# Leftover rows of two experts in one tile of an expert layer

## The chip, the cores and the metric

The kernel runs on one core of a Trainium2 chip. The metric is the device time of one execution in microseconds, here the median of three timed runs; beside them one execution was taken by the hardware profiler. The engines are named as the profile does: PE is TensorE's matmuls, PEld its weight loads, DVE VectorE, ACT ScalarE, POOL GpSimd, SP SyncE, and a q behind a name is that engine's queue.

## The reference

Three layers follow each other: a gated linear attention over 4 batches, 8 heads, 768 steps and 48 numbers a head; a SiLU layer of 384 to 2048 to 384 on the 3072 tokens; and a layer of 8 experts in which each token goes to the one expert with the highest score. The last is what the change touches:

```python
N, D, E, F = (3072, 384, 8, 1024)
expert_idx = np.argmax(logits, axis=1)
for e in range(E):
    mask = expert_idx == e
    h = np.maximum(x[mask] @ w1[e], 0.0)
    out[mask] = gate_w[mask, None] * (h @ w2[e])
```

## The kernel before

Every product of the two matmul layers is made of three fp16 products (high by high, high by low, low by high), so that it is nearly as exact as fp32. The attention, the SiLU layer and the conversion of all weights run first, interleaved, up to about 600 us. All expert weights then lie in SBUF as pairs of fp16 (`w1s`, `w2s`).

`route` (line 900) scores 128 tokens at a time and scatters each token's row into a DRAM buffer `xs_d` in which every expert has a region of its own: the row as two halves of fp16, and ten numbers of metadata (its place in the output, its scale, eight scores). The expert layer then works on tiles of 128 rows of one expert each. Eight tiles (`KEARLY`) are listed by `early` (line 1085) from the tokens routed before the last block, whole tiles only. `tile_list` (line 1096) lists the others when all tokens are counted: `tiles_of` rounds each expert's remaining rows up to whole tiles, and `listing` makes the first row (`idx`) and the expert (`ei`) of 23 places; places past the end of the list point to dummy rows. An expert's last tile is thus partly empty: its rows past the end are padding (`write_pads`, line 1112) that the output scatter leaves out.

29 tiles (`NSTAT`, 8 + 21) always run; two more are behind a branch (line 1357) that is entered when the list is longer than 21 (`extra`, line 1103). A tile goes through these steps:

- `prep_load` (line 1125): SyncE loads the first row's number into a register (line 1130), transposes the 128 rows from DRAM into `xT` (line 1135, three buffers) and loads the metadata `mt` (line 1136, four buffers).
- `prep_fac` (line 1145): the softmax weight of each row, on ACT and DVE.
- `expert1` (line 1165), once for each half of 1024 hidden columns: PE makes nine matmuls of 512 columns into `hp` (line 1183), 18 a tile, with the rows as the stationary operand and the expert's weights streaming; ACT and DVE split the result into two fp16 parts (lines 1189, 1190); `send` (line 1161) has SyncE transpose them back into SBUF. The destinations are `g3` and `hb` for even tiles and two parts of `work` for odd ones.
- `expert2` (line 1196): 24 matmuls of 384 columns into `po` (line 1209), 12 from each half of the hidden columns; ACT scales the result (line 1217) and GpSimd scatters the rows into the output (line 1220).

The expert of a tile is in a register of PE, so each matmul's weights are addressed at run time. In the loop of line 1340, turn j issues the load of tile j+3, the weights of rows of tile j+2, the first stage of tile j+1 and the second stage of tile j. The order on each engine is set when the program is built, by a planner that runs the instructions through a model of their times and picks, among those that are ready, the earlier one in the code. The queues work strictly in that order; a SyncE instruction that waits holds up all behind it.

Of the kernel before, what the change touches and what calls it, by code (L numbers as in the profile page):

```python
# [272 lines left out]
def attention_silu_moe_kernel(  # L273
# [14 lines left out]
    nc = tc.nc  # L288
    B, H, S, D = q.shape
    NT, DM = out.shape  # L290
# [11 lines left out]
    AHEAD = 2  # L302
    POOLW2 = {(c, e) for c in range(4, KE) for e in (0, 4)}
    GATE = mybir.DependencyClass.Sync
    NLIST = NTILE - KEARLY
    NSTAT = NTILE - 2
    CAP = NT + 128
    DUMMY = E * CAP
    ROW = DM + E + 2
# [11 lines left out]

    def guard(kind, thr=0.0, op=ALU.is_lt):
        if kind not in guards:
            width = {"decay": 2 * NCH, "nat": NCH, "finite": 160}.get(kind, 16)
            t = const.tile([128, width], FP32, name=f"guard_{kind}")
            nc.vector.memset(t, 2.0 * thr if op == ALU.is_lt else 0.0)
            guards[kind] = [t, 0, thr, op]
        g = guards[kind]
        g[1] += 1
        return g[0][:, g[1] - 1:g[1]]  # L330
# [41 lines left out]
    if True:  # L372
# [662 lines left out]
        es = const.tile([128, E], FP32, name="es")  # L1035
        idx0 = const.tile([128, KEARLY], I32, name="idx0")
        ei0 = const.tile([128, KEARLY], I32, name="ei0")
        idx = const.tile([128, NLIST], I32, name="idx")
        ei = const.tile([128, NLIST], I32, name="ei")
        ends = const.tile([128, E], I32, name="ends")  # L1040
        extra = const.tile([128, 1], I32, name="extra")
# [54 lines left out]
        def tile_list():  # L1096
            cn = totals(NCH, "cn1")
            nc.vector.scalar_tensor_tensor(
                out=ends, in0=iota8, scalar=float(CAP), in1=cn, op0=ALU.mult, op1=ALU.add
            )  # L1100
            nc.vector.tensor_sub(out=cn, in0=cn, in1=es)
            tl, tcum = tiles_of(cn, 127.0)
            nc.vector.tensor_scalar(
                out=extra, in0=tcum[:, E - 1:E], scalar1=float(NSTAT - KEARLY), scalar2=None, op0=ALU.is_gt
            )
            base = m2.tile([128, E], FP32, tag="base", name="base1", bufs=1)
            nc.vector.scalar_tensor_tensor(out=base, in0=iota8, scalar=float(CAP), in1=es, op0=ALU.mult, op1=ALU.add)
            listing(tl, tcum, base, NLIST, idx, ei)

        early_loads, pads = [], []  # L1110

# [10 lines left out]

        tl_ = {}

        def prep_load(j):
            d = tl_[j] = {}
            d["x"] = xT = m2.tile([128, 2 * KD, 128], FP16, tag="row", name="xT", bufs=3)
            mt = m2.tile([128, ROW - DM], FP32, tag="mt", name="mt", bufs=4)
            src = idx0[0:1, j:j + 1] if j < KEARLY else idx[0:1, j - KEARLY:j - KEARLY + 1]
            r = nc.values_load(  # L1130
                src, engines=sp, min_val=0, max_val=DUMMY,
                skip_runtime_bounds_check_because="a tile starts inside an expert's rows or at the dummy rows",
            )
            loads = [
                nc.sync.dma_start_transpose(out=xT, in_=xs_d.bitcast(FP16)[bass.ds(r, 128), 0:2 * DM]),
                nc.sync.dma_start(out=mt, in_=xs_d[bass.ds(r, 128), DM:]),
            ]
            if j < KEARLY:
                for ins in loads:
                    for other in scattered[NCH - TPB:] + pads:  # L1140
                        tc.declare_no_dep(ins.ins, other.ins, reason="early tiles hold tokens of earlier blocks only")
                early_loads.extend(loads)
            d["m"] = mt
# [21 lines left out]
        def expert1(j, i, keep=False):  # L1165
            d = tl_[j]
            if i == 0:
                d["e"] = nc.values_load(
                    ei0[0:1, j:j + 1] if j < KEARLY else ei[0:1, j - KEARLY:j - KEARLY + 1],
                    engines=[mybir.EngineType.PE], min_val=0, max_val=E - 1,  # L1170
                    skip_runtime_bounds_check_because="the chip clamps the index to an expert",
                )
                d["hs"] = work[:, 1024 * (j % 2):1024 * (j % 2 + 1)].bitcast(FP16).rearrange(
                    "p (i s f) -> p i s f", i=2, s=2)
                odd = work[:, 2048:3072].bitcast(FP16)
                d["hT"] = (odd[:, 0:1024], odd[:, 1024:2048]) if j % 2 else (g3[:, 0:1024], hb)
            xT = d["x"]
            fs = slice(i * 512, (i + 1) * 512)
            hp = ps_h.tile([128, 512], FP32, tag="h", name="hp2")
            n = 0  # L1180
            for c in range(KD):
                for a, w in ((c, "h"), (KD + c, "h"), (c, "l")):
                    nc.tensor.matmul(  # L1183
                        out=hp, lhsT=xT[:, a, :], rhs=w1s[w][c][:, bass.ds(d["e"], 1), fs],
                        start=(n == 0), stop=(n == 3 * KD - 1),
                    )
                    n += 1
            hs = d["hs"][:, i]
            nc.scalar.activation(out=hs[:, 0], in_=hp, func=ACTF.Relu)  # L1189
            nc.vector.scalar_tensor_tensor(  # L1190
                out=hs[:, 1], in0=hp, scalar=0.0, in1=hs[:, 0], op0=ALU.max, op1=ALU.subtract
            )
            if not keep:
                send(j, i)

        def expert2(j, part=None):
            d = tl_[j] if part == 0 else tl_.pop(j)
            hT = d["hT"]
            if part != 1:
                d["o"] = (  # L1200
                    bank([128, 512], FP32, "po") if j < 2 else ps_o.tile([128, 512], FP32, tag=f"o{j % 2}", name="po")
                )[:, 0:DM]
            po = d["o"]
            order = [[0, 1, 2, 3], [4, 5, 6, 7]] if part is None else [[[0, 1, 2, 3], [4, 6]], [[5, 7]]][part]
            n, total = (3 * 6 if part == 1 else 0), 3 * KE
            for group in order:
                for a, w in ((0, "h"), (0, "l"), (4, "h")):
                    for c in group:
                        nc.tensor.matmul(
                            out=po, lhsT=hT[c // 4][:, (a + c % 4) * 128:(a + c % 4 + 1) * 128], rhs=w2s[w][c][:, bass.ds(d["e"], 1), :],  # L1210
                            start=(n == 0), stop=(n == total - 1),
                        )
                        n += 1
            if part == 0:
                return
            ob = m2.tile([128, ROW], FP32, tag="sq", name="ob", bufs=1)[:, 0:DM]
            nc.scalar.activation(  # L1217
                out=ob, in_=po, func=ACTF.Copy, scale=d["fac"], accum_out=guard("finite", 0.0, ALU.not_equal)
            )
            nc.gpsimd.indirect_dma_start(  # L1220
                out=out[:, :], out_offset=bass.IndirectOffsetOnAxis(ap=d["row"], axis=0),
                in_=ob, in_offset=None, bounds_check=NT - 1, oob_is_err=False,
            )
# [113 lines left out]
        send(3, 1)  # L1337
        tile_list()
        write_pads()
        for j in range(2, NSTAT):  # L1340
            if j + 3 < NSTAT:
                prep_load(j + 3)
            if j + 2 < NSTAT:
                prep_fac(j + 2)
            if 2 < j and j + 1 < NSTAT:
                expert1(j + 1, 0)
                expert1(j + 1, 1)
            if j + 2 == NSTAT:
                bad = const.tile([128, len(guards) + 1], FP16, name="bad")
                n_fin = guards["finite"][1]  # L1350
                for i, kind in enumerate(guards):
                    check(i, kind, 0, guards[kind][1])
            expert2(j)
# [1 line left out]
    more = nc.values_load(extra[0:1, 0:1], min_val=0, max_val=NTILE,  # L1355
                          skip_runtime_bounds_check_because="at most NTILE tiles in the list")
    with tc.If(more > 0):
        for j in range(NSTAT, NTILE):
            prep_load(j)
            prep_fac(j)  # L1360
            expert1(j, 0)
            expert1(j, 1)
            expert2(j)
# [43 lines left out]
```

## Time and profile before

| | us |
|---|---|
| median of 3 timed runs (838.42 to 839.84) | 839.2 |
| the profiled execution | 834.05 |
| its span, first to last instruction | 832.4 |

The page of the profile gives, for each engine, the busy time and its share of the span, and in 40 slices of the span the busy tenths (9 is 90% or more) and TensorE's granted clock in tenths of full speed. The views of the trace used below are the table by stretches (busy time of each engine in a stretch), the timeline (instructions in order, equal neighbours merged, with a count at the end), the groups by line, and the waits. Matmuls follow each other before the one ahead has ended, so the duration of one is longer than the distance between two.

### The profile page before, as it was taken

The numbers are of one execution on the slowest core, as the hardware profiler recorded it, in microseconds if no ns is written. First come the engines' busy times: TensorE is split into PE (matmuls) and PEld (weight loads), VectorE is DVE, ScalarE is ACT, GpSimd is POOL, SyncE is SP. The second block draws the span as 40 slices with busy tenths as digits, with TensorE's granted clock in tenths as the row PEclk, the third lists the DMA queues.
The fourth block names the chain that finished last, engine by engine and source line by source line (L and its number), as shares of the span: only waits on it lengthen the run. The fifth ranks groups of instructions, "written<-read, shape, count | busy, mean of one in ns | idle before, by whom it ended". The sixth has DMA issues, their size and how long they took to land. (4 is left out here: it accounts for less than half of the span.)

```text
span 832.4 us, 16583 instructions
## 1 busy us (share of the span) xinstructions
PE 779.0 (94%) x5488; PEld 492.0 (59%) x5488; DVE 500.0 (60%) x1444; ACT 431.4 (52%) x931; POOL 248.2 (30%) x335
## 2 busy tenths in 40 slices
PE   6879799999999999998999988989799999999996
PEld 5756577667667666665657655555344555555553
DVE  7799963767777977786677576466543222222221
ACT  2456664656675846666556575667542222222221
POOL 3342311534453554444222121131343111111111
PEclk9959899999999999999999999999999999999998
DMA  9997132144445454534521345345588666555663
GB/s 188 256 289 201 48 49 48 50 93 80 96 106 118 89 147 100 112 96 86 106 79 47 97 135 159 90 134 153 166 160 188 115 112 121 103 118 120 109 117 61
DMA packets 244028, 98.66 MB, mean 119 GB/s; under 512 B 224969, under 2 KB 233326, under 8 KB 243808
## 3 DMA queue, kind: packets, MB, share of 16 engines
q1 hardware_dynamic: 240288, 86.31, 48.8%
q0 software_dynamic: 3648, 11.18, 3.9%
q8 instruction: 51, 0.84, 0.4%
q14 instruction: 41, 0.34, 0.1%
HBM read 58.40 MB, written 12.36 MB: 85 GB/s over the span
## 5 line engine op out<-in xcount | busy, mean ns | idle before, releaser
L870 PE MATMUL hp<-w2h,wi_h 128*128 128x384 f16 x576 | 146.2, 331 | 7.4 <-ACT w2l L877 5.3
L893 PE MATMUL o<-wo_h,w2l 128*128 128x392 f16 x528 | 147.1, 333 | 6.0 <-DVE wo_h L569 3.6
L1190 DVE SCALAR_TENSOR_TENSOR work<-hp,work 128x512 f16<-128x512 f32 x58 | 39.9, 690 | 121.6 <-ACT work L1189 121.5
L893 PEld LDWEIGHTS <-w2l 128*128 128x128 f16 x792 | 75.5, 98 | 57.9 <-issue 6.9
L870 PEld LDWEIGHTS <-wi_h 128*128 128x128 f16 x768 | 74.0, 98 | 54.7 <-issue 10.1
L1183 PE MATMUL hp<-w1h,xT 128*128 x348 | 103.5, 379 | 2.4 <-DVE work L1190 2.4
L870 PE MATMUL hp<-w2h,wi_l 128*128 128x384 f16 x288 | 94.8, 330 | 0.1
L893 PE MATMUL o<-wo_l,w2l 128*128 128x392 f16 x264 | 87.8, 332 | 0.0
L1183 PEld LDWEIGHTS <-xT 128*128 128x128 f16 x522 | 50.9, 98 | 60.7 <-issue 3.0
L1220 POOL DMA_INDIRECT out_dram<-ob,mt x29 | 28.3, 976 | 176.3 <-ACT ob L1217 171.7
L1189 ACT ACTIVATE work<-hp 128x512 f16<-128x512 f32 x58 | 34.4, 595 | 68.4 <-PE hp L1183 61.6
L893 PE MATMUL o<-wo_h,g 128*128 128x392 f16 x240 | 67.0, 329 | 1.2 <-DVE g L879 1.1
L879 DVE SCALAR_TENSOR_TENSOR w2l<-w2l 128x384 f16<-128x384 f32 x88 | 51.1, 583 | 27.8 <-ACT w2l L878 27.5
L1183 PE MATMUL hp<-w1l,xT 128*128 x174 | 66.0, 379 | 0.0
L877 ACT ACTIVATE w2l<-hp 128x384 f32<-128x384 f32 x88 | 42.4, 483 | 36.0 <-PE hp L870 31.8
L692 PE MATMUL sc<-Q,K 64*128 64x128 f32 x384 | 54.8, 307 | 1.7 <-DVE state L817 1.0
L692 PEld LDWEIGHTS sc<-Q,K 64*128 64x128 f32 x384 | 46.0, 207 | 14.0 <-issue 7.1
L870 PEld LDWEIGHTS <-wi_l 128*128 128x128 f16 x384 | 37.8, 99 | 24.3 <-issue 1.0
L698 POOL TENSOR_SCALAR_AFFINE_SELECT S<-S 128x512 f32<-128x512 f32 x48 | 36.5, 764 | 45.7 <-ACT S L697 45.3
L878 ACT ACTIVATE w2l<-w2l 128x384 f16<-128x384 f32 x88 | 45.7, 521 | 5.8 <-PE o L893 4.1
L870 PE MATMUL hp<-w2l,wi_h 128*128 128x384 f16 x192 | 48.2, 326 | 0.0
L893 PEld LDWEIGHTS <-g 128*128 128x128 f16 x360 | 34.0, 98 | 23.2 <-DVE g L879 2.2
(276 smaller groups left out, 1603.7 us busy)
## 6 DMA issues: line engine op xcount, KB each, us to landing
work<-in_moe_w_dram SPq DMA_DIRECT2D x24, 512.0 KB, 3.8
work<-in_moe_w_dram SPq DMA_DIRECT2D x30, 384.0 KB, 3.5
w1h<-in_moe_w_in_dram SPq DMA_DIRECT2D x6, 768.0 KB, 5.4
nat_a<-in_alpha_dram SPq DMA_DIRECT2D x23, 192.0 KB, 3.2
nat_k<-in_k_dram SPq DMA_DIRECT2D x23, 192.0 KB, 2.8
nat_q<-in_q_dram SPq DMA_DIRECT2D x23, 192.0 KB, 3.2
nat_v<-in_v_dram SPq DMA_DIRECT2D x23, 192.0 KB, 2.9
w1h<-in_moe_w_out_dram SPq DMA_DIRECT2D x5, 768.0 KB, 7.2
```

The lines of the kernel that those rows point to most:

```text
L692: nc.tensor.matmul(out=sc[i][:, p, :], lhsT=d["K"][r, p, :], rhs=d["Q"][r, p, :], start=True, stop=True)
L698: nc.gpsimd.affine_select(out=s, in_=s, pattern=[[0, NPAIR], [1, 128]], compare_op=ALU.is_ge, fill=0.0, base=0, channel_multiplier=-1,)
L870: ins = nc.tensor.matmul(out=hp, lhsT=wi[a][f // 2][:, c, (f % 2) * 128:(f % 2 + 1) * 128], rhs=x[:, c, :], start=(n == 0), stop=(n == 3 * ...
L877: nc.scalar.activation(out=g, in_=hp, func=ACTF.Silu, scale=1.0 / (SX * SWI))
L878: nc.scalar.activation(out=gh, in_=g, func=ACTF.Copy, scale=SG)
L879: lead["g"] = nc.vector.scalar_tensor_tensor(out=gl, in0=g, scalar=SG, in1=gh, op0=ALU.mult, op1=ALU.subtract)
L893: nc.tensor.matmul(out=acc[t], lhsT=a[:, ts], rhs=wo[w][f // 2][:, f % 2, :], start=(f == 0 and n == 0), stop=(f == KF - 1 and n == 2),)
L1183: nc.tensor.matmul(out=hp, lhsT=xT[:, a, :], rhs=w1s[w][c][:, bass.ds(d["e"], 1), fs], start=(n == 0), stop=(n == 3 * KD - 1),)
L1189: nc.scalar.activation(out=hs[:, 0], in_=hp, func=ACTF.Relu)
L1190: nc.vector.scalar_tensor_tensor(out=hs[:, 1], in0=hp, scalar=0.0, in1=hs[:, 0], op0=ALU.max, op1=ALU.subtract)
L1220: nc.gpsimd.indirect_dma_start(out=out[:, :], out_offset=bass.IndirectOffsetOnAxis(ap=d["row"], axis=0), in_=ob, in_offset=None, bounds_ch ...
```

## The change

Tiles become whole only where more than 64 rows are left: `tiles_of` rounds with 63 in place of 127. The 64 or fewer rows that an expert has left go to a shared tile, four of which exist, for experts 0 and 1, 2 and 3, 4 and 5, 6 and 7. In a shared tile rows 0 to 63 belong to the one expert and rows 64 to 127 to the other. Each of its matmuls is two: each has half of the columns of the stationary operand, streams the weights of its own expert, and writes its half of the partitions of the same PSUM bank. These experts are known when the program is built. 24 whole and 4 shared tiles always run, the shared ones last; up to three whole tiles are behind the branch (entered when the list is longer than 16). The loads of a shared tile are two for each kind, of 64 rows, each with a register of its own. The number of the buffers that alternate from tile to tile (`s`) follows the order of running. Tables of guards that have at most 8 entries get 8 places.

```diff
-    NLIST = NTILE - KEARLY
-    NSTAT = NTILE - 2
+    NFULL = (NT + 63 * E) // 128
+    NLIST = NFULL - KEARLY
+    SFULL, SPAIR = NCH, E // 2
...
-            tl, tcum = tiles_of(cn, 127.0)
+            tl, tcum = tiles_of(cn, 63.0)
...
-            listing(tl, tcum, base, NLIST, idx, ei)
+            listing(tl, tcum, base, NLIST, idx[:, 0:NLIST], ei)
+            nc.vector.scalar_tensor_tensor(out=cn, in0=tl, scalar=-128.0, in1=cn, op0=ALU.mult, op1=ALU.add)
+            nc.vector.tensor_scalar(out=cn, in0=cn, scalar1=0.0, scalar2=None, op0=ALU.is_gt)
+            nc.vector.scalar_tensor_tensor(out=base, in0=tl, scalar=128.0, in1=base, op0=ALU.mult, op1=ALU.add)
+            nc.vector.scalar_tensor_tensor(
+                out=base, in0=base, scalar=float(-DUMMY), in1=cn, op0=ALU.add, op1=ALU.mult
+            )
+            nc.vector.tensor_scalar(out=idx[:, NLIST:], in0=base, scalar1=float(DUMMY), scalar2=None, op0=ALU.add)
...
+        def parts(j):
+            if j < KEARLY:
+                return [(slice(0, 128), idx0[0:1, j:j + 1], ei0[0:1, j:j + 1])]
+            if j < NFULL:
+                n = j - KEARLY
+                return [(slice(0, 128), idx[0:1, n:n + 1], ei[0:1, n:n + 1])]
+            cols = [2 * (j - NFULL) + h for h in range(2)]
+            return [
+                (slice(64 * h, 64 * h + 64), idx[0:1, NLIST + e:NLIST + e + 1], e) for h, e in enumerate(cols)
+            ]
...
+            for ts, src, _ in parts(j):
+                r = nc.values_load(
...
+                size = ts.stop - ts.start
+                loads += [
+                    nc.sync.dma_start_transpose(out=xT[:, :, ts], in_=xs_d.bitcast(FP16)[bass.ds(r, size), 0:2 * DM]),
+                    nc.sync.dma_start(out=mt[ts], in_=xs_d[bass.ds(r, size), DM:]),
+                ]
...
-                    nc.tensor.matmul(
-                        out=hp, lhsT=xT[:, a, :], rhs=w1s[w][c][:, bass.ds(d["e"], 1), fs],
-                        start=(n == 0), stop=(n == 3 * KD - 1),
-                    )
+                    for ts, e in d["e"]:
+                        nc.tensor.matmul(
+                            out=hp[ts], lhsT=xT[:, a, ts], rhs=w1s[w][c][:, e if isinstance(e, int) else bass.ds(e, 1), fs],
+                            start=(n == 0), stop=(n == 3 * KD - 1),
+                        )
...
+                        at = (a + c % 4) * 128
+                        for ts, e in d["e"]:
+                            nc.tensor.matmul(
+                                out=po[ts], lhsT=hT[c // 4][:, at + ts.start:at + ts.stop],
+                                rhs=w2s[w][c][:, e if isinstance(e, int) else bass.ds(e, 1), :], start=(n == 0), stop=(n == total - 1),
+                            )
...
-        for j in range(2, NSTAT):
-            if j + 3 < NSTAT:
-                prep_load(j + 3)
...
+        order = [*range(SFULL), *range(NFULL, NFULL + SPAIR)]
+        for n in range(2, len(order)):
+            j = order[n]
+            if n + 3 < len(order):
+                prep_load(order[n + 3])
...
-        for j in range(NSTAT, NTILE):
+        for j in range(SFULL, NFULL):
```

## Rows read from the trace of the kernel before

**Rows 1.** The page: TensorE's busy time, its slices, its granted clock.

```profile
PE 779.0 (94%) x5488; PEld 492.0 (59%) x5488; DVE 500.0 (60%) x1444; ACT 431.4 (52%) x931; POOL 248.2 (30%) x335
PE   6879799999999999998999988989799999999996
PEclk9959899999999999999999999999999999999998
```

**Rows 2.** Table by stretches: engines' busy us (instructions), PE clock, DMA share, GB/s.

```profile
640.00:823.90 183.90, 183.88 (x996) 97.23 (x995) 44.56 (x115) 50.10 (x138) 23.32 (x24) 1.00 0.61 113
```

**Rows 3.** Timeline, 760 to 785: start us, us, what; weight loads of two tiles.

```profile
765.53 3.71 PEld L1183 LDWEIGHTS <-xT 128*128 128x128 f16 x18
...
769.36 3.89 PEld L1209 LDWEIGHTS <-work 128*128 128x128 f16 x24
...
773.32 3.71 PEld L1183 LDWEIGHTS <-xT 128*128 128x128 f16 x18
...
781.10 3.71 PEld L1183 LDWEIGHTS <-xT 128*128 128x128 f16 x18
```

**Rows 4.** Tile xT, 640 to 824: duration in ns, least, median and longest.

```profile
L1183 PEld LDWEIGHTS <-xT x414: 95/98/98, 640.7 to 815.9; 128*128 128x128 f16 x138
```

**Rows 5.** Timelines of TensorE by windows in 455 to 465: line 692's halves, line 619.

```profile
461.43 0.49 PE L692 MATMUL sc<-Q,K 64*128 64x128 f32 x4
...
461.43 0.60 PE L692 MATMUL sc<-Q,K 64*128 64x128 f32 x6
...
461.43 1.16 PE L692 MATMUL sc<-Q,K 64*128 64x128 f32 x16
462.53 0.34 PE L893 MATMUL o<-wo_h,w2l 128*128 128x392 f16 x1
...
461.43 0.97 PEld L692 LDWEIGHTS sc<-Q,K 64*128 64x128 f32 x16
...
455.71 0.60 PE L619 MATMUL ptr<-ident,nat_k 128*128 128x128 f32 x4
```

**Rows 6.** Groups of VectorE by form, 600 to 833: the tile list's operations, wide and small.

```profile
L1073 DVE TENSOR_TENSOR g<-g,tl 128x184 f32<-128x184 f32 x1 | 0.3, 349 | 0.0
...
L1055 DVE TENSOR_SCALAR ci<-cn 128x8 int32<-128x8 f32 x1 | 0.2, 172 | 0.0
```

**Rows 7.** Timeline, 815 to 833: the tail.

```profile
823.44 0.81 PE L1209 MATMUL po<-w2h,hb 128*128 x4
824.34 0.58 ACT L1217 ACTIVATE ob<-po,s 128x384 f32<-128x384 f32 x1 [3.23 <-PEq L1357]
```

**Rows 8.** Timeline of SyncE's queue, 648 to 664.

```profile
653.00 0.34 SPq L1136 DMA_DIRECT2D mt<-xs_d  x1
653.44 1.23 SPq L1161 DMA_TRANSPOSE work<-work  x1
655.72 1.23 SPq L1135 DMA_TRANSPOSE xT<-xs_d  x1
657.05 1.25 SPq L1161 DMA_TRANSPOSE work<-work  x1
660.82 0.34 SPq L1136 DMA_DIRECT2D mt<-xs_d  x1
```

**Rows 9.** Line 1130, 640 to 824: register loads on SyncE, ns as in rows 4.

```profile
L1130 SPq TENSOR_LOAD <-idx x21: 278/811/841, 641.9 to 794.9; - x21
```

**Rows 10.** Waits of SyncE's queue, 660 to 825: us in total, times, longest.

```profile
SPq L1136 <- DMA out_dram<-ob,mt: 40.4, 19, 2.6
```

**Rows 11.** Line 1161, 640 to 824: from a returning transpose's issue to its landing.

```profile
DMA to landing us min/median/max: 3.0/3.2/4.9
```

**Rows 12.** Timeline, 648 to 664: the second return's data; the block that uses it.

```profile
653.43 0.69 DVE L1190 SCALAR_TENSOR_TENSOR work<-hp,work 128x512 f16<-128x512 f32 x1 [1.25 <-ACT work L1189]
...
660.17 3.89 PEld L1209 LDWEIGHTS <-work 128*128 128x128 f16 x24
```

**Rows 13.** Timeline of TensorE, 636 to 640: a wait for a returning transpose.

```profile
638.96 0.82 PE L1209 MATMUL po<-w2h,hb 128*128 x4 [1.20 <-DMA hb<-work]
```

More of the change, by code (lines that the diff above doesn't have):

```diff
@@ L323, in guard @@
         if kind not in guards:
-            width = {"decay": 2 * NCH, "nat": NCH, "finite": 160}.get(kind, 16)
+            width = {"decay": 2 * NCH, "nat": NCH, "finite": 160}.get(kind, 8)
             t = const.tile([128, width], FP32, name=f"guard_{kind}")
@@ L1037, in attention_silu_moe_kernel @@
         ei0 = const.tile([128, KEARLY], I32, name="ei0")
-        idx = const.tile([128, NLIST], I32, name="idx")
+        idx = const.tile([128, NLIST + E], I32, name="idx")
         ei = const.tile([128, NLIST], I32, name="ei")
@@ L1101, in tile_list @@
             nc.vector.tensor_sub(out=cn, in0=cn, in1=es)
-            tl, tcum = tiles_of(cn, 127.0)
+            tl, tcum = tiles_of(cn, 63.0)
             nc.vector.tensor_scalar(
-                out=extra, in0=tcum[:, E - 1:E], scalar1=float(NSTAT - KEARLY), scalar2=None, op0=ALU.is_gt
+                out=extra, in0=tcum[:, E - 1:E], scalar1=float(SFULL - KEARLY), scalar2=None, op0=ALU.is_gt
             )
@@ L1123, in attention_silu_moe_kernel @@
         tl_ = {}
+        def parts(j):
[8 more added lines that the diff above has]
+            ]
         def prep_load(j):
-            d = tl_[j] = {}
+            d = tl_[j] = {"s": (j - NFULL + SFULL if j >= NFULL else j) % 2}
             d["x"] = xT = m2.tile([128, 2 * KD, 128], FP16, tag="row", name="xT", bufs=3)
             mt = m2.tile([128, ROW - DM], FP32, tag="mt", name="mt", bufs=4)
[L1129 to L1132, printed above, removed]
-            )
[L1134 to L1137, printed above, removed]
+            loads = []
+            for ts, src, _ in parts(j):
+                r = nc.values_load(
+                    src, engines=sp, min_val=0, max_val=DUMMY,
+                    skip_runtime_bounds_check_because="a tile starts inside an expert's rows or at the dummy rows",
+                )
[4 more added lines that the diff above has]
+                ]
             if j < KEARLY:
@@ L1167, in expert1 @@
             if i == 0:
[L1168 to L1173, printed above, removed]
+                d["e"] = [
+                    (ts, src if isinstance(src, int) else nc.values_load(
+                        src, engines=[mybir.EngineType.PE], min_val=0, max_val=E - 1,
+                        skip_runtime_bounds_check_because="the chip clamps the index to an expert",
+                    )) for ts, _, src in parts(j)
+                ]
+                s = d["s"]
+                d["hs"] = work[:, 1024 * s:1024 * (s + 1)].bitcast(FP16).rearrange(
                     "p (i s f) -> p i s f", i=2, s=2)
                 odd = work[:, 2048:3072].bitcast(FP16)
-                d["hT"] = (odd[:, 0:1024], odd[:, 1024:2048]) if j % 2 else (g3[:, 0:1024], hb)
+                d["hT"] = (odd[:, 0:1024], odd[:, 1024:2048]) if s else (g3[:, 0:1024], hb)
             xT = d["x"]
@@ L1182, in expert1 @@
                 for a, w in ((c, "h"), (KD + c, "h"), (c, "l")):
-                    nc.tensor.matmul(
-                        out=hp, lhsT=xT[:, a, :], rhs=w1s[w][c][:, bass.ds(d["e"], 1), fs],
-                        start=(n == 0), stop=(n == 3 * KD - 1),
-                    )
+                    for ts, e in d["e"]:
[3 more added lines that the diff above has]
+                        )
                     n += 1
@@ L1200, in expert2 @@
                 d["o"] = (
-                    bank([128, 512], FP32, "po") if j < 2 else ps_o.tile([128, 512], FP32, tag=f"o{j % 2}", name="po")
+                    bank([128, 512], FP32, "po") if j < 2 else ps_o.tile([128, 512], FP32, tag=f"o{d['s']}", name="po")
                 )[:, 0:DM]
@@ L1208, in expert2 @@
                     for c in group:
[L1209 to L1212, printed above, removed]
+                        at = (a + c % 4) * 128
[3 more added lines that the diff above has]
+                                rhs=w2s[w][c][:, e if isinstance(e, int) else bass.ds(e, 1), :], start=(n == 0), stop=(n == total - 1),
+                            )
                         n += 1
@@ L1339, in attention_silu_moe_kernel @@
         write_pads()
-        for j in range(2, NSTAT):
-            if j + 3 < NSTAT:
-                prep_load(j + 3)
[L1343 to L1348, printed above, removed]
+        order = [*range(SFULL), *range(NFULL, NFULL + SPAIR)]
[3 more added lines that the diff above has]
+                prep_load(order[n + 3])
+            if n + 2 < len(order):
+                prep_fac(order[n + 2])
+            if 2 < n and n + 1 < len(order):
+                expert1(order[n + 1], 0)
+                expert1(order[n + 1], 1)
+            if n + 2 == len(order):
                 bad = const.tile([128, len(guards) + 1], FP16, name="bad")
```

## The prediction, made before the change was timed

> **What bounds the kernel now.** The page comes first: TensorE is busy for 94% of the span, in nearly every slice, at close to its full clock [rows 1]. In the last stage, the expert tiles, this hardens: from 640.00 to 823.90 us TensorE is busy 183.88 of 183.90 us at a granted clock of 1.00, which is 2.4 GHz, while VectorE, ScalarE and GpSimd each stay below 30% [rows 2]. So the stage has one limit, and the timeline shows it as a rhythm: a tile is a block of 18 weight loads of line 1183, then one of 24 of line 1209, and the blocks of line 1183 begin at 765.53, 773.32 and 781.10 us [rows 3], 7.79 and 7.78 us apart. I use 7.785 us. The block of line 1209 begins at 769.36, so each stage has about half of it, 3.89 us: 0.216 us for each of 18 matmuls of 512 columns, 0.162 us for each of 24 of 384. The loads lie under the matmuls: 98 ns each [rows 4], 42 of them would be 4.1 us a tile, and there is no idle time to hold them. A tile fewer is therefore worth 7.785 us, as long as nothing else becomes late.
>
> **What the change takes away.** 29 tiles always run; afterwards 24 whole and 4 shared ones do. Five whole tiles go: 5 x 7.785 = 38.9 us, all of it on TensorE's path. For this the branch at the end must not be entered. Counted from the reference's inputs, the experts have 415, 398, 420, 336, 406, 321, 384 and 392 rows; the early list takes two tiles (256 rows) of each of the first four, which leaves 159, 142, 164, 80, 406, 321, 384 and 392. Rounded up, as before, that is 2+2+2+1+4+3+3+4 = 21 tiles for 21 places. Rounded up only above 64 left over it is 1+1+1+1+3+3+3+3 = 16 for 16 places (80 and 321 = 256 + 65 round up; 31, 14, 36, 22 and 8 rows go to the shared tiles). Full, but not over, so the branch stays shut.
>
> **What four shared tiles cost on TensorE.** Each issues 2 x 42 matmuls, one half writing partitions 0 to 63, the other 64 to 127, each streaming 512 or 384 columns of its own expert. Side by side, a pair costs what one matmul costs; one after the other, twice that. No row of before shows column halves. The nearest are the scores of line 692, two matmuls at a time on separate halves of 64 rows: four of them take 0.49 us and six 0.60 us, so one more pair costs 0.11 us; four unpaired matmuls of as many fp32 columns (line 619) take 0.60 us, one of them 0.27, so (0.60 - 0.27)/3 = 0.11 us each [rows 5]. Row halves do run side by side, and a pair costs what a single one costs within the 0.01 us of the rows; I take 3 ns, so 42 x 3 ns = 0.13 us a tile, 7.91 us for a shared tile. The bounds are 7.785 and twice that (a rival, below); the row nearest in kind, halves in pairs, stands at the low end, so I stay there. Changing shape costs too: the second pair begins 0.49 - 0.27 = 0.22 us after the first instead of 0.11, and the next full matmul begins at 462.53, 0.21 us behind the last pair's start (461.43 + 1.16 - 0.27 = 462.32) [rows 5]: 0.1 us a change. The second stage of the last whole tile lies between the first stages of the first two shared ones, so there are three changes: 0.3 us. Together 4 x 7.91 + 0.3 = 31.9 us.
>
> Then the weight loads. In whole tiles a load goes to the same 128 rows as the matmul in flight and is hidden [rows 2 to 4]; in line 692 two loads a pair are hidden as well, 16 of them within 0.97 us [rows 5]. I cost the 84 shorter loads of a shared tile at nothing; their cover is the pair's own 0.162 to 0.216 us. A rule of the Trainium skill speaks against the change here: TensorE: Matmul & The Clock Gate, Part 3, says that a load overlaps a matmul in flight only when it goes to another group of rows, and halves by columns share their rows. The trace does not agree for whole tiles; by the rule the loads would stand open, which is the third rival.
>
> **What else moves.** The tile list gets five operations on 8 numbers at 0.17 us and does its seven wide ones on 152 instead of 184 numbers, 0.35 us each before [rows 6]: +0.85 less some 0.4 us on VectorE. The first load that needs the list (tile 8, the first of 21) is at 641.9 us [rows 9], for a tile that TensorE reaches four tiles later, so I cost this at nothing; without that cover it is 0.5 us. The exponential, the guard sums and the scatter stay one per tile, and PE's register work for a shared tile goes, which was hidden. The tail from the last matmul (guard check, branch, last scatter) is the same for any last tile [rows 7].
>
> The one queue that gets more work is SyncE's. Its turn for a whole tile: metadata load at 653.00, a transpose that returns hidden values (line 1161) at 653.44, a register load (0.81 us [rows 9]), the transpose of rows (line 1135) at 655.72, the second return from 657.05 to 658.30; then it stands until 660.82 [rows 8], because the metadata's buffer comes free only when an earlier tile's scatter has landed (40.4 us in 19 waits [rows 10]). So 5.3 of 7.8 us are work. A shared tile adds a register load, a transpose of 64 rows and a metadata load of 0.34 us: with gaps 2.5 us if the half transpose costs as much as a whole one, 1.9 us if half. I take 2.5, since the duration hardly follows the size: 1.23 us for 6 blocks of 128 x 128 and 1.23 to 1.25 for 8 [rows 8]. The queue becomes just full in the four turns that load shared tiles. The loads are three tiles early; what can hurt is the second return, queued behind them. Issued at 657.05 it lands 3.2 us later [rows 11], at 660.25, and is needed in the second half of the block that begins at 660.17 [rows 12], 12 of 24 loads on, at 662.1: 1.9 us in hand. Behind the new register load and transpose (2.2 us) and the second metadata load (0.4 us) it is 0.7 us late; with these in the 2.5 us in which the queue stands anyway, it isn't. The second return has its data from VectorE at 653.43 + 0.69 = 654.12 [rows 12], before the first row transpose is through, and it stands earlier in the code than the loads of the next turn, so I take the second order, with 0.2 us in all for the full queue.
>
> **The sum.** -38.9 + 31.9 + 0.2 = -6.8 us. Against the profiled execution (span 832.4 us, outside it 834.05 - 832.4 = 1.65 us) that is 827.2 us. The median of the three timed runs, 839.2, lies 5.15 us above that execution; I carry this over: 839.2 - 6.8 = 832.4 us.
>
> **Rivals.** (1) *SyncE's queue gives part of it back.* With the other order the second return is 0.7 us late at the median landing, 2.4 at the longest (4.9 us [rows 11]), in four turns: 2.8 to 9.6 us, most likely 3: 835.4, up to 842. For it: the full queue, and that such a wait stood once already, 1.20 us for hb at 638.96 [rows 13]. Against it: the idle 2.5 us.
> (2) *The halves run one after the other.* 4 x 2 x 7.785 = 62.3 for 38.9 us: +23.4, 862.6 us. A shared tile loses from 38.9/4 = 9.7 us on, a quarter above a whole one. For it: a column half streams 128 partitions of its own, while the halves of line 692 share them out, 64 each; nothing in before shows two such streams at once. Against it: those pairs.
> (3) *The weight loads come into the open.* 84 a tile at 98 ns [rows 4] are 8.2 us, half of that if half the columns cost half: +16.5 to +33 us for four tiles beside the gain of 6.8, so 849 to 865 us. Against it: every hidden load of before.
> (4) *It isn't what runs*: the list overflows and the branch adds tiles one by one, over 7.785 us each: 840 and more. Against it: the counts.
>
> **How the numbers follow.** The forecast with its sides, 830.8 to 834: 0.62. Rival 1: 0.20. Rival 2: 0.07. Rival 3: 0.06. Rival 4, or a planner that orders the work before 640 us differently, to either side: 0.05. A measurement can tell about 0.2%, 1.7 us, from no change: 837.5 to 840.9 is "same". Of rival 1, 0.17 lies below that. Faster: 0.62 + 0.17 + 0.03 = 0.82; same 0.05; slower 0.07 + 0.06 = 0.13. The range goes down to nothing for pairs, shape changes and queue (-7.8 with no premium, 831.4) less 0.6 us for the timed runs, which lie 1.4 us apart, and up over most of rival 1, to 837.5; outside lie the rest of it and the serial cases, under 0.2.
>
> **What would show it.** Right: in shared tiles two matmuls of line 1183 that begin within some ns, blocks 7.9 us apart, 28 blocks, no wait of TensorE for work, g or hb behind 700 us. Rival 1: such waits in the second stages of the last whole and of the shared tiles. Rival 2: 0.43 us from pair to pair. Rival 3: TensorE idle before its matmuls until a load ends. Wrong altogether: the branch entered, or another order before 640 us.

## The result and the profile after

| | before | after |
|---|---|---|
| device time, median | 839.52 us (4 runs, 838.42 to 841.26) | 829.25 us (4 runs, 826.75 to 830.51) |
| ratio after/before, 95% interval | | 0.9872 [0.9842, 0.9902] |
| profiled execution, its span | 834.05, 832.4 us | 830.51, 828.9 us |

The change makes the kernel 1.3% faster. The forecast was 832.4 us in a range of 830.8 to 837.5: the direction holds, the size doesn't, and the time lies 1.55 us below the low end. Two more measurements of the same kernel, further down, gave ratios of 0.9901 and 0.9877. The mean of the three is 0.9883, 9.8 us on 840 instead of the 6.8 forecast.

The page of the changed kernel (TensorE's busy time, slices, granted clock), against [rows 1]:

```profile
PE 774.7 (93%) x5614; PEld 489.7 (59%) x5614; DVE 497.4 (60%) x1444; ACT 428.6 (52%) x925; POOL 246.0 (30%) x334
...
PE   6879799999999999999899989989788999999996
...
PEclk9659799999999999999999999999999999999999
```

The 126 matmuls more (5614 - 5488) are what four shared tiles add and five whole ones take, 4 x 84 - 5 x 42: the branch stays shut.

The table by stretches, from 640 us to the end of the last expert matmul, against [rows 2]: us, then busy us and instructions of PE, PEld, DVE, ACT and POOL, PE clock, DMA share, GB/s.

```profile
640.00:820.70 180.70, 179.46 (x1126) 96.32 (x1127) 43.14 (x113) 48.39 (x135) 22.34 (x23) 0.99 0.61 112
```

TensorE is still the limit of the stage, but no longer without a gap: 1.2 us are missing, where before 0.02 were. The timeline of weight loads shows the last whole tile and the first shared ones, against [rows 3]:

```profile
779.58 1.94 PEld L1235 LDWEIGHTS <-g 128*128 128x128 f16 x12
781.58 1.89 PEld L1235 LDWEIGHTS <-hb 128*128 128x128 f16 x12
783.78 3.59 PEld L1207 LDWEIGHTS <-xT 128*64 128x64 f16 x36 [0.32 <-issue]
787.79 3.69 PEld L1235 LDWEIGHTS <-work 128*128 128x128 f16 x24 [0.41 <-issue]
791.80 3.59 PEld L1207 LDWEIGHTS <-xT 128*64 128x64 f16 x36 [0.32 <-issue]
795.49 1.96 PEld L1235 LDWEIGHTS <-g 128*64 128x64 f16 x24
798.50 1.77 PEld L1235 LDWEIGHTS <-hb 128*64 128x64 f16 x24 [1.05 <-DMA hb<-work]
800.32 3.73 PEld L1207 LDWEIGHTS <-xT 128*64 128x64 f16 x36
805.00 3.72 PEld L1235 LDWEIGHTS <-work 128*64 128x64 f16 x48 [0.95 <-DMA work<-work]
808.76 3.73 PEld L1207 LDWEIGHTS <-xT 128*64 128x64 f16 x36
```

A block of a shared tile has twice the loads of a whole one and takes as long: 36 loads in 3.73 us from 800.32, where 18 took 3.71 [rows 3]. The matmuls on TensorE's timeline say the same (start, us, what; `128*64` is a half of the columns):

```profile
779.14 0.59 PE L1207 MATMUL hp<-w1h,xT 128*128 x2
779.58 0.38 PE L1207 MATMUL hp<-w1l,xT 128*128 x1
...
784.46 0.60 PE L1207 MATMUL hp<-w1h,xT 128*64 128x512 f16 x4
784.89 0.38 PE L1207 MATMUL hp<-w1l,xT 128*64 128x512 f16 x2
785.11 0.60 PE L1207 MATMUL hp<-w1h,xT 128*64 128x512 f16 x4
```

Four halves take 0.60 us where two whole matmuls take 0.59, and one group of two pairs and one pair begins 0.65 us after the other, 0.217 us a pair. So the halves run beside each other. What is new are the two waits, for `hb` and for `work` (1.05 and 0.95 us of the weight loads, 0.7 and 0.5 us of the matmuls): both are transposes that return through SyncE's queue. This queue from 786 us on, against [rows 8], and then VectorE's operations that make the data of `g` and of the first `work`:

```profile
786.16 2.85 SPq L1156 DMA_TRANSPOSE xT<-xs_d  x2
789.31 1.52 SPq L1157 DMA_DIRECT2D mt<-xs_d  x2
790.95 1.49 SPq L1182 DMA_TRANSPOSE g<-work  x1
793.49 1.19 SPq L1156 DMA_TRANSPOSE xT<-xs_d  x1
794.78 1.32 SPq L1182 DMA_TRANSPOSE hb<-work  x1
797.32 1.18 SPq L1156 DMA_TRANSPOSE xT<-xs_d  x1
798.76 1.18 SPq L1157 DMA_DIRECT2D mt<-xs_d  x2
800.05 2.76 SPq L1182 DMA_TRANSPOSE work<-work  x2
```
```profile
786.59 0.69 DVE L1214 SCALAR_TENSOR_TENSOR work<-hp,work 128x512 f16<-128x512 f32 x1 [1.79 <-ACT work L1213]
794.60 0.69 DVE L1214 SCALAR_TENSOR_TENSOR work<-hp,work 128x512 f16<-128x512 f32 x1 [0.95 <-ACT work L1213]
```

A transpose of 64 rows costs the queue 1.18 to 1.19 us (a whole one 1.23 [rows 8]). Before, one metadata load stands ahead of a tile's first return and one row transpose between its two returns [rows 8]. Here two row transposes and two metadata loads stand ahead of `g`, which goes at 790.95 though its data were ready at 787.28 (786.59 + 0.69); another row transpose follows, and `hb` goes at 794.78. It lands at 798.5, when the block that uses it has already stood for 1.05 us. The returns of `work`, the first of which had its data at 795.29, go from 800.05 on, behind one more row transpose and two metadata loads. The queue, which stood for 2.5 us of a turn before, has no such pause here: its two gaps of over 1 us, before 793.49 and 797.32, hold a register load each (line 1150, up to 1.04 us).

### The profile page after: what moved, and what is told of

It is laid out like the page before. It is cut to its first block, busy times and chain, and to the rows that moved or that the text cites. A ratio compares the mean times of both kernels' runs of the same rounds, so it can differ in the third digit from the quotient of the medians.

```text
span 828.9 us, 16620 instructions
## 1 busy us (share of the span) xinstructions
PE 774.7 (93%) x5614; PEld 489.7 (59%) x5614; DVE 497.4 (60%) x1444; ACT 428.6 (52%) x925; POOL 246.0 (30%) x334
## 5 line engine op out<-in xcount | busy, mean ns | idle before, releaser
L1207 PE MATMUL hp<-w1h,xT 128*128 (+1 forms) x384 | 102.2, 385 | 2.9 <-DVE work L1214 2.9
L1207 PEld LDWEIGHTS <-xT 128*128 128x128 f16 (+1 forms) x576 | 50.8, 102 | 60.6 <-issue 8.0
L1207 PE MATMUL hp<-w1l,xT 128*128 (+1 forms) x192 | 64.7, 384 | 0.0
```

The lines of the kernel that those rows point to most:

```text
L1207: nc.tensor.matmul(out=hp[ts], lhsT=xT[:, a, ts], rhs=w1s[w][c][:, e if isinstance(e, int) else bass.ds(e, 1), fs], start=(n == 0), stop=( ...
```

## The experiments

All were timed beside the kernel before on the same chip. Besides the ratio, two places of each trace are compared: the stretch from the first weight load of tile 9, in the order of running from 0 (line 1183, 1207 in the changed kernel), to the start of the last expert matmul, where only the tiles run; and the start of the first expert matmul, before which both kernels do the same work. With the unchanged kernels these are the yardstick:

| kernel | median us | ratio [95%] | tile 9 to end, us | first expert matmul at |
|---|---|---|---|---|
| before, profiled first | 839.2 | | 159.8 | 583.1 |
| b_again (before) | 839.06 | 0.9986 [0.9961, 1.0011] | 160.2 | 587.5 |
| b_more (before) | 840.22 | 0.9992 [0.9966, 1.0017] | 160.0 | 587.6 |
| after, profiled first | 829.25 | 0.9872 [0.9842, 0.9902] | 154.0 | 582.9 |
| a_again (after) | 832.09 | 0.9901 [0.9865, 0.9936] | 154.2 | 580.1 |
| a_more (after) | 830.47 | 0.9877 [0.9847, 0.9907] | 155.5 | 582.6 |

> The kernel before, unchanged, timed against itself on the chip of the runs beside it and profiled again. Tile theory (the change is worth 6.8 us, and the rest of the 10.3 us measured is a difference between executions that the change has no part in): ratio 1.000 within 0.002; its span comes out 3 to 5 us above the 832.4 us of the first profile, and the surplus lies before 650 us, in waits of TensorE for transposes, not in the rhythm of 7.785 us a tile. Rival, list theory (the shorter tile list or the freed memory make the work before 650 us faster): the span is again 832 to 833, and 'after' beside it is 10 us faster with 3 us of that before its eighth tile begins.

> The changed kernel, unchanged, on the same chip as the kernel before beside it. Tile theory: 6 to 7.5 us below b_again's runs (ratio 0.991 to 0.993); from the start of tile 8 to the last matmul it takes 6.0 us less than b_again (7.785 less 0.3 for three changes of shape less 1.5 us of waits seen in the first profile). List theory: 10 us below, ratio 0.988, 3 us of it before tile 8.

> The changed kernel again, for more executions of it and one more profile. Spread theory: over all its timed runs it comes nearer to -7 us (ratio 0.990 to 0.993), and the profile shows the stage from tile 8 on 5 to 6 us shorter than before, again with one or two waits for returning transposes at the shared tiles. Layout or list theory: it stays at -9 to -10 us (ratio 0.988 to 0.990), with a tile 8 that begins 2 to 3 us sooner on average.

> The kernel before, unchanged. Both theories: ratio 0.998 to 1.002. Halves theory: first expert matmul at 586 to 588.5 us; chance theory: anywhere between 580 and 588.

The stage falls by some 5.5 us, the time by 9.8, and the work before the stage, which the change doesn't touch, ends some 4 us earlier (the clock has a part in the single places, see the section on the buffers). So two questions: why the stage gave less than forecast, and where the rest comes from.

**The price of a tile: t28 and a_one.** t28 is the kernel before with one always-running tile less (28 whole; the 8 rows of the last are left out). a_one is the changed kernel with each shared tile computed as one whole tile of its first expert (experts 1, 3, 5 and 7 lose their leftover rows).

```diff
-    NSTAT = NTILE - 2
+    NSTAT = NTILE - 3
...
```
```diff
-                (slice(64 * h, 64 * h + 64), idx[0:1, NLIST + e:NLIST + e + 1], e) for h, e in enumerate(cols)
+                (slice(0, 128), idx[0:1, NLIST + e:NLIST + e + 1], e) for h, e in enumerate(cols[:1])
```

> The kernel before with 28 whole tiles in place of 29 and nothing else changed; the last tile of the list, 8 rows, is left out. Tile theory: 7.8 us below b_again (ratio 0.9907), so 0.5 to 2 us below a_again. List theory: 7.8 us below b_again too, but a_again is 2 to 3 us faster than this one.

> The changed kernel, but a shared tile is computed as one whole tile of its first expert: one load, 42 matmuls; the leftover rows of experts 1, 3, 5 and 7 are left out. 28 whole tiles with the new list. Tile theory: as t28 within 1 us, and 1.5 to 2 us below a_again: 0.3 us of shape changes, up to 0.5 us of pairs, 1.5 us of waits behind the second loads. List theory: as a_again less 1 us, so 2 us below t28.

> The changed kernel with each shared tile computed as one whole tile of its first expert, run again (the rows of the second experts are left out). Halves theory: first expert matmul at 586 to 588.5 us again and ratio 0.990 to 0.992. Chance theory (the places of 583 and 587 us are chance of single executions): first expert matmul anywhere between 580 and 588, ratio 0.986 to 0.989 as the changed kernel's, less the queue's 2 us.

t28: 834.74, ratio 0.994 [0.9916, 0.9965], tile 9 to end 152.3 us. a_one: 832.62, 0.9906 [0.9874, 0.9938], 152.7; again (a_one2) 829.0, 0.9873 [0.9826, 0.9919], 151.8. The mean, 152.3, is 7.7 us below the 160.0 of before: one tile, as forecast. t28 gives back some 2.5 us in the tail, where the matmul of the guard check (line 1366) waits for TensorE's sequencer. Timelines of the tail, of b_more first, then t28:

```profile
831.86 0.10 PEld L1366 LDWEIGHTS <-ones 128*128 128x128 f16 x1 [0.67 <-issue]
833.16 0.17 PE L1366 MATMUL pb<-bad,ones 128*128 128x10 f16 x1 [1.58 <-DVE bad L1233]
```
```profile
827.68 0.10 PEld L1366 LDWEIGHTS <-ones 128*128 128x128 f16 x1 [3.92 <-issue]
827.72 0.17 PE L1366 MATMUL pb<-bad,ones 128*128 128x10 f16 x1 [3.56 <-PEq L1357]
```

**The halves: a_ser and b_half.** a_ser issues all matmuls of one half before those of the other, in each accumulation. b_half is the kernel before with its last four whole tiles computed as two halves of the last expert, whose rows they hold (the expert is then a constant of the code, as in the shared tiles).

```diff
-            for c in range(KD):
-                for a, w in ((c, "h"), (KD + c, "h"), (c, "l")):
-                    for ts, e in d["e"]:
+            for ts, e in d["e"]:
+                n = 0
+                for c in range(KD):
+                    for a, w in ((c, "h"), (KD + c, "h"), (c, "l")):
...
```
```diff
+        def halves(j):
+            return [slice(0, 64), slice(64, 128)] if NSTAT - 4 <= j < NSTAT else [slice(0, 128)]
...
+                    for ts in halves(j):
+                        nc.tensor.matmul(
+                            out=hp[ts], lhsT=xT[:, a, ts], rhs=w1s[w][c][:, d["e"], fs],
...
```

> The changed kernel, but in each accumulation all matmuls of the first half are issued before all of the second half, so neighbours in the stream are on the same half. Theory that halves overlap only with the neighbour in the stream: a shared tile takes 15.6 us in place of 7.9, and the whole 4 x 7.7 = 31 us more, some 862 us. Rival (the halves are queued separately and overlap whatever the order): as the changed kernel, 830 us. Between them, the ends of the sequences could overlap by one matmul: 30 us more.

> The kernel before with its last four whole tiles computed as two column halves each, both of the last expert (whose rows these tiles hold); nothing else differs. Sum theory: halves cost 0.1 us per change of shape and nothing else, so the time is that of before to +0.5 us (ratio 1.000 to 1.001), with the first matmul of the expert tiles at 586 to 588.5 us. Halves theory (running column halves makes the work before tile 8 of the same kernel earlier, by whatever way): 3 to 4 us less, ratio 0.995 to 0.996, first expert matmul at 582 to 584.5 us.

a_ser: 841.81 us, ratio 1.0006 [0.9979, 1.0033], 11 us above the changed kernel; the 31 us of fully serial halves did not come either. Its timeline shows why:

```profile
782.55 0.62 PE L1207 MATMUL hp<-w1h,xT 128*64 128x512 f16 x2
783.01 0.38 PE L1207 MATMUL hp<-w1l,xT 128*64 128x512 f16 x1
783.23 0.59 PE L1207 MATMUL hp<-w1h,xT 128*64 128x512 f16 x2
783.66 0.38 PE L1207 MATMUL hp<-w1l,xT 128*64 128x512 f16 x1
783.66 0.81 PE L1207 MATMUL hp<-w1h,xT 128*64 128x512 f16 x4
784.12 0.56 PE L1207 MATMUL hp<-w1l,xT 128*64 128x512 f16 x2
```

The first half begins at 782.55; at 783.66, after five matmuls alone, the second begins although the first has four of its nine left, and for these four both run (x4 in 0.81 us, x2 in 0.56). A run of nine in one half so costs 1.11 us instead of 1.94. So alternating the halves in the code isn't needed to make them overlap, but it is what makes the overlap complete.

b_half: 839.64, ratio 1.0003 [0.9977, 1.0028], tile 9 to end 160.5: halves cost 0.5 us in four tiles. That its time is that of before says that running halves is not what makes the work ahead of the tiles earlier.

**The queue: a_ld1 and a_pool.** a_ld1 loads a shared tile's rows and metadata with one load of 128 rows each (so rows 64 to 127 are not the second expert's). a_pool is the complete kernel with the metadata loads from tile 8 on issued by GpSimd, so that their waits for the scatter leave SyncE's queue too.

```diff
-            for ts, src, _ in parts(j):
+            for ts, src, _ in parts(j)[:1]:
+                ts = slice(0, 128)
```
```diff
-                    src, engines=sp, min_val=0, max_val=DUMMY,
+                    src, engines=sp if j < KEARLY else sp + [mybir.EngineType.Pool], min_val=0, max_val=DUMMY,
...
-                    nc.sync.dma_start(out=mt[ts], in_=xs_d[bass.ds(r, size), DM:]),
+                    (nc.sync if j < KEARLY else nc.gpsimd).dma_start(out=mt[ts], in_=xs_d[bass.ds(r, size), DM:]),
```

> The changed kernel, halves in the matmuls kept, but the 128 rows of a shared tile are loaded in one transpose and one metadata load from the first expert's place; so rows 64 to 127 are not the second expert's. Queue theory (the second loads make the returning transposes late): no wait of TensorE at the shared tiles, from tile 8 on 1.5 to 2 us shorter than the changed kernel, that is 7.3 to 7.6 us shorter than before. Rival (the waits come from the halves on TensorE or from the row transposes' 64-row shape itself and not from the queue): the waits stay or the stage is less than 0.5 us shorter.

> The changed kernel, but from tile 8 on the metadata loads of all tiles are issued by GpSimd in place of SyncE, so a shared tile puts two transposes and two register loads more on SyncE's queue and no metadata, and the wait for the scatter leaves that queue too. Queue theory (the returning transposes of the shared tiles are late because SyncE's queue is full): no waits of TensorE at the shared tiles, from tile 8 to the last matmul 160.0 to 160.5 us, 1.5 to 2.5 below the changed kernel, ratio 0.985 to 0.988. Rival (GpSimd's own issue and its waits delay the scatter and the exponentials instead): new waits of ScalarE's line for the exponential, and the stage no shorter.

> The changed kernel with the metadata loads from tile 8 on issued by GpSimd, again. Queue theory: 1 to 3 us below the changed kernel, ratio 0.983 to 0.988; halves theory: first expert matmul at 582 to 584.5 us; chance theory: anywhere between 580 and 588.

a_ld1: 830.24, 0.9855 [0.9822, 0.9888], tile 9 to end 152.5. a_pool: 827.63, 0.9838 [0.981, 0.9866], 152.5; again (a_pool2) 829.74, 0.9868 [0.9833, 0.9903], 152.4. TensorE's waits from 700 us on (us in total, times, longest), of the changed kernel, then of a_pool:

```profile
PE pb L1394 <- DVE bad L1259: 1.6, 1, 1.6
PE po L1235 <- DMA hb<-work: 0.7, 1, 0.7
PE po L1235 <- DMA work<-work: 0.5, 1, 0.5
```
```profile
PE pb L1394 <- DVE bad L1259: 1.6, 1, 1.6
PE po L1235 <- SPq L1385: 0.2, 1, 0.2
```

With less on SyncE's queue both waits go and the stage takes 152.45 us, as with 28 whole tiles. The changed kernel's 154.5 (mean of its executions above and of a_pad, 154.3) are 2.0 us more: that is the queue's price (1.55 in the first profile, of which the two waits are 1.2; the rest was not taken apart). In both runs a row transpose still stands between a tile's two returns (at 793.36 us in a_ld1, at 787.94 in a_pool), and neither shows such a wait: a row transpose between the returns doesn't make them late by itself. What counts is how much stands on the queue. a_pool is the fastest kernel here: the mean of its two ratios is 0.985.

**The rest: b_g8, b_pad, b_pad3, a_pad.** Three things that the change also alters: the size of the guard tables (b_g8: 8 places in the kernel before), and the code in the branch that is not entered (one or three more tiles' code in before, three more in after).

```diff
-            width = {"decay": 2 * NCH, "nat": NCH, "finite": 160}.get(kind, 16)
+            width = {"decay": 2 * NCH, "nat": NCH, "finite": 160}.get(kind, 8)
```
```diff
-        for j in range(NSTAT, NTILE):
+        for j in [*range(NSTAT, NTILE), *[NTILE - 1] * 3]:
```

> The kernel before with the one edit that the guard tables have 8 places in place of 16; all later data in SBUF move by some hundred bytes, nothing else changes. Spread theory (executions of one program differ by 4 us to either side before tile 8, the change has no part in that): ratio 1.000 within 0.003. Layout theory (the shifted addresses make the work before tile 8 faster, which is the 2 to 3 us of the change that the tile rhythm doesn't explain): 2 to 3 us below before, ratio 0.997 or less.

> The kernel before with one more tile's code behind the branch that is never entered: nothing that runs is changed, the program is longer by about as much as that of the changed kernel. Placement theory (the 3 us or so by which the changed kernel is faster before its tile 8 come from where the longer program lies, not from anything that it does): 3 us below before, ratio 0.996 to 0.997, first matmul of line 1183 near 583 us in place of 587. Chance theory (they are chance): ratio 1.000 within 0.0025.

> As b_pad with three more tiles' code behind the branch. Placement theory: again off by 2 us or more, to either side. Chance theory: ratio 1.000 within 0.0025.

> The changed kernel with three more tiles' code behind the branch that is never entered. Placement theory: it moves against the changed kernel by 2 us or more, to some -6 us against before (ratio 0.993). Chance theory, and a theory by which the shared tiles themselves make the work before them faster: as the changed kernel, ratio 0.987 to 0.990.

b_g8 839.83, 0.9988 [0.9965, 1.0011]; b_pad 840.98, 0.9995 [0.9971, 1.002]; a_pad 832.62, 0.9899 [0.9872, 0.9926]: none accounts for 4 us. b_pad3 is slower, 845.51, 1.0041 [1.0021, 1.0062], but at the other end: from the end of the last expert weight load to the end of the span it takes 13.3 us instead of 8.1 to 8.8, and the check's matmul waits as in t28 (in a_pad too, for 2.2 us). Code size alone doesn't settle this (b_pad has as many tiles in its branch as t28, and no such wait); its cause stays open.

**Where buffers lie: b_al and a_mis.** What the traces then showed is a wait in the attention part, 100 to 580 us, where the order of work is the same: TensorE waits for `KT`, a transpose through SyncE's queue (line 729, 730 in the changed kernel). The view of that line up to 600 us: the transposes (duration on the queue in ns, first and last start), TensorE's waits for them (us, times), and the time from issue to landing; of before, then of after:

```profile
L729 SPq DMA_TRANSPOSE KT<-kd x14: 1231/1232/1247, 165.3 to 395.1; - x14
...
  PE up L799: 4.8, 4
...
DMA to landing us min/median/max: 3.1/3.2/5.0
```
```profile
L730 SPq DMA_TRANSPOSE KT<-kd x14: 1232/1233/1248, 166.8 to 393.1; - x14
...
  PE up L800: 3.0, 3
...
DMA to landing us min/median/max: 2.7/2.7/4.5
```

The issue takes as long, the landing 0.5 us less. The wait is 4.0 to 4.8 us in all eight traces of kernels built on before, 2.5 to 3.1 in all ten built on the changed one. What differs is the place: the narrower guard tables (192 bytes less) and the longer list `idx` (27 places instead of 23, 32 bytes more) move `KT`, `kd` and `ys`, and with them nearly all that lies behind the tables, down by 160 bytes in each partition, `KT` from byte 110240, 32 past a multiple of 64, to 110080, a multiple of 64. b_g8 moves it to 110048, again 32 past. b_al and a_mis move it by 32 bytes with a longer guard table: b_al puts before's buffers where the changed kernel has them, a_mis puts the changed kernel's 32 past.

```diff
-            width = {"decay": 2 * NCH, "nat": NCH, "finite": 160}.get(kind, 16)
+            width = {"decay": 2 * NCH, "nat": NCH, "finite": 168}.get(kind, 8)
```
```diff
-            width = {"decay": 2 * NCH, "nat": NCH, "finite": 160}.get(kind, 8)
+            width = {"decay": 2 * NCH, "nat": NCH, "finite": 168}.get(kind, 8)
```

> The kernel before with guard tables of 8 places, as b_g8, and one table 8 places longer: KT, kd and ys then start on multiples of 64 bytes, at the very addresses of the changed kernel; 29 whole tiles, nothing else differs. Placement theory: a KT transpose lands 2.7 to 2.8 us after its issue instead of 3.2, TensorE waits 2.5 to 3.1 us for KT instead of 4.0 to 4.8, and the time falls by 1.5 to 3.5 us, ratio 0.996 to 0.998. Chance theory: waits of 4.0 to 4.8 us, ratio 0.998 to 1.002 as b_g8's.

> The changed kernel with one guard table 8 places longer, so that KT, kd and ys start 32 bytes past a multiple of 64, as in the kernel before; nothing else differs. Placement theory: landings of 3.2 us, waits for KT of 4.0 to 4.8 us, and 1.5 to 3.5 us more than the changed kernel, ratio 0.991 to 0.994. Chance theory: waits of 2.5 to 3.1 us and the ratio of the unchanged kernel, 0.987 to 0.990.

TensorE's waits for `KT` from 100 to 580 us (us in total, times, longest), in b_al, then in a_mis:

```profile
PE up L799 <- DMA KT<-kd: 2.6, 3, 2.1
```
```profile
PE up L800 <- DMA KT<-kd: 4.3, 4, 2.5
```

b_al: 838.47, 0.9983 [0.9957, 1.001], first expert matmul at 579.9. a_mis: 835.73, 0.9947 [0.9919, 0.9976], first expert matmul at 587.1, tile 9 to end 154.4. The wait follows the place in both directions. So does the transpose: a matmul that waits for `KT` begins 2.76 to 2.79 us after its issue in b_al and 3.17 to 3.24 in a_mis (one in each later, 4.47 and 4.92), and in all twenty traces these are 2.75 to 2.85 us on a multiple of 64 and 3.09 to 3.27 at 32 past.

What the place is worth in time is less sure. a_mis gives back about half of the gain: 0.9947 against 0.9883 is 5.4 us. b_al alone, 1.4 us with an interval that takes in no change, would not show it by its time. Over all traces the first expert matmul stands at 586.4 us on average in the nine that have these buffers 32 past (583.1 to 588.7) and at 582.9 in the eleven that have them on a multiple (579.9 to 587.1), 3.5 us apart, between the two timed values. The clock has a part in these places. In some executions it rises earlier, as the table by stretches shows for the first 100 us of before and of b_again (the third number from the end is the granted clock):

```profile
0.00:100.00 100.00, 78.62 (x505) 59.65 (x506) 89.13 (x199) 51.72 (x94) 38.71 (x59) 0.85 0.87 202
```
```profile
0.00:100.00 100.00, 75.47 (x480) 57.32 (x481) 87.73 (x194) 49.89 (x89) 38.34 (x59) 0.78 0.87 202
```

Among the traces with 0.78 there the two places are 3.9 us apart (587.5 in six, a_mis one of them, and 583.6 in seven), among those with 0.85 or 0.86 1.8 us (583.4 in two, 581.7 in four, b_al one of them); b_pad, at 0.80, is in neither group. And not all goes with the place: a_one and a_one2 have the buffers on a multiple and short waits for `KT`, 3.1 and 3.0 us, and yet their first expert matmul comes at 587.1 and 583.6 us, the latest on a multiple at either clock. 1.7 us of the 3.5 are the wait for `KT` itself; how the others divide was not taken apart. The `ys` transposes, whose source moves too, land in 2.5 to 2.6 us instead of 2.8. 110080 is a multiple of 512 as well, so the runs don't show from which multiple on a buffer lies well.

## Why the prediction was wrong

- *A whole tile is worth 7.785 us*: right, 7.7.
- *Column halves run side by side, a pair for one; 0.3 us for the changes of shape; loads hidden*: right. 0.5 us for all in b_half, 0.2 in a_ld1 and a_pool against 28 whole tiles; forecast were 0.8 with the pairs' 3 ns, which don't add up (a pair follows the one before after 0.217 us, as a whole matmul does). Rivals 2 and 3 fell. Of rival 3's rule (the Trainium skill, TensorE: Matmul & The Clock Gate, Part 3: a load overlaps a matmul in flight only when it goes to another group of rows) the trace of the changed kernel shows the opposite for halves too: 36 loads to the same rows within a block of 3.73 us, and no idle time for them.
- *The queue costs 0.2 us, since the second return goes ahead of the new loads, which find room in the 2.5 us in which the queue stands*: wrong, 2.0 us. The price of a half transpose was right (1.19 of 1.23 us), the room and the order were not: two row transposes and two metadata loads stand ahead of the first return already, the queue doesn't stand in these turns, and two returns are late. This is rival 1 in kind, and its 3 us was the better size.
- *The rest is as before*: wrong, and this is what put the time out of the range; the 5.5 us of the stage alone would have been inside. The narrowing of the guard tables stands in the diff and has no line in the sum; it changed nothing by itself (b_g8), but with the longer `idx` it moves the buffers of the attention part, and TensorE's waits for `KT` follow that place (b_al, a_mis). By the starts of the first expert matmul it is worth some 3.5 us, about half of the forecast gain; timed, 1.4 and 5.4 us, so its size is known to some 2 us only, and beyond the 1.7 us of the wait for `KT` the cause of it stays open. Stage and place together, 5.5 + 3.5 = 9.0 us, come to the 9.8 measured, within the 1.5 us that three such intervals leave.
- *The range went 0.6 us below the sum's own bound, for the 1.4 us between the timed runs*: too narrow. Executions of the unchanged kernel, 139 in all the comparisons here, lie between 834.6 and 846.1 us.

Without the shift of the buffers the time would by this have been some 1.3 us above the forecast (an estimate: 6.8 - 5.5); the two errors have opposite signs, and the larger one was in a line of the diff that looked like housekeeping.

## What to carry to other kernels

Two half-filled tiles of different weights can share one pass when each takes a half of TensorE's columns and their matmuls alternate: a pair costs what one matmul costs, and the price is on the queue that loads the extra rows, where a half load costs about as much as a whole one (1.19 of 1.23 us). Where a change resizes any table, compare the addresses of what lies behind it: here a DMA transpose between buffers that lie 32 bytes past a multiple of 64 landed 0.4 to 0.5 us later than between buffers on a multiple (of 512, as it happens), in every trace. Take the range's width from many executions of the unchanged kernel, not from three.

## What the runs showed of the hardware

- Column halves run beside each other (four in 0.60 us, two whole matmuls in 0.59), and TensorE goes on to the other half while the first still has four matmuls to finish (a_ser: 1.11 us for a run of nine, 1.94 if they waited).
- `KT`'s transpose: 2.7 us from issue to landing with its buffers on a multiple of 64 (110080, which is one of 512 too), 3.2 us at 32 past (three such places), with the same 1.23 us on the queue.
- A transpose of 64 rows takes 1.18 to 1.19 us of SyncE's queue, one of 128 rows 1.23.
- The time of an execution goes with the granted clock of its span: of the 139 executions of the kernel before, the 38 with a mean granted clock of up to 0.964 average 842.7 us, the 32 with 0.970 and more 838.6.
